# VectorE's order pinned in the attention loops, weight slabs fetched one step ahead, longer spacing in the finish of a group

## The chip, the cores and the metric

The program runs on one core of a Trainium2 chip. Its time is the device time of one execution in microseconds (us). The engines of the core run side by side and wait for each other through semaphores: TensorE (PE) does matmuls and transposes through PSUM, VectorE (DVE) and ScalarE (ACT) do elementwise work, GpSimd (POOL) does a little, and SyncE (SP) issues nearly all DMAs.

## The reference

Four layers run one after the other on x of 2048 tokens by 576 features, in f32: A, B, A, B, each with a residual and a layer norm before it. The two A layers share weights, and so do the two B layers.

```python
def A(x):                                   # attention, one K and one V head for 32 query heads of 18
    q = (x @ wq) per head; k = x @ wk; v = x @ wv
    p = softmax(q k^T * 18**-0.5)           # 32 heads x 2048 x 2048
    return (p v, heads joined) @ wo
def B(x):                                   # linear attention with a learned feature map
    q, k, v = x @ wqkv, 32 heads of 18
    phi(y) = [softmax(y w_phi), softmax(-y w_phi)]          # 36 features
    kv = phi(k)^T v;  z = sum of phi(k)
    return (phi(q) kv / (phi(q) z + 1e-6)) @ wo
x = x + A(norm(x)); x = x + B(norm(x)); x = x + A(norm(x)); x = x + B(norm(x))
```

## The kernel before

**Two attention loops with other work mixed in.** The kernel calls an A layer with the B layer behind it a "layer", so there are two. `attend` holds the loop of one layer. Tokens are cut into 4 chunks of 512 queries, heads into 8 groups of 4. A pair (chunk, group) is one *group* of the loop; the first of 32 is done before the loop, 31 in it. For each group and each of 16 key tiles the loop makes two units: scores of two heads (L451, tile `sc`), their exponential on ScalarE (L963, tile `pt`), and then the product with V, four matmuls (L741). So a group has 32 units, the loop 992.

**The step.** While there is other work ("bulk"), one pass of the loop, here called a step, takes 6 units: `scores(3)`, the sums that are ready, two calls of `tick()`, `scores(3)`, one call of `fill()`, the sums that are ready unless the fill was heavy, and a third `tick()`. `fill()` runs the bulk generator up to the end of one projection (14 matmuls, L205) or up to a `yield STAGE`, which gives the turn back. A step without bulk also takes 6 units and three ticks. 165 steps and a third make the loop.

**The bulk.** For each finished chunk `chunk_work` does 8 projections with `wo` (`output`, residual added by VectorE at L262, `flip_tokens` on VectorE), then `mix` over 4 token tiles: keys b0, b1, values b0, b1, queries b0, b1 (six projections) and `update_state`, 32 small matmuls (L526; the profile counts an f32 matmul twice, so 64 there) whose result VectorE adds to `kv` (L532). After a projection of keys or queries VectorE runs five instructions (`feature_start`, L482 to L487) and ScalarE one exponential (L489); `feature_end` (L494 to L496) normalizes, and the features are block-transposed (L576) and spilled. So a chunk is 36 fills, and 3 of the 4 chunks are done inside the loop; the last follows behind it. In layer 0 the loop's first bulk is `fold_phi`.

**One spare bank.** The loop has two PSUM banks beside those for scores, tags `acc` and `ps`. One collects the group's sum; the other, `Spare`, takes every projection and the state update. When a group ends, the two change places (`homes.reverse()`). So a projection can begin only when VectorE has read the one before it out of the spare bank, and a new group's first sum needs that bank empty too.

**What a tick does.** A tick advances three generators by one `yield`: `urgent` (the finish of a group), `loads` (weight slabs) and `slow` (spills). The finish of a group (`finish_group`): VectorE copies the sums to `osb` (L873); a DMA brings the softmax denominators into `rd`; VectorE takes reciprocals (L881); a DMA writes them to DRAM (`den_rows`), another reads them back spread over the heads (`parts`); VectorE multiplies (L891) and splits the result into a high and a low part; `pack` (L822) moves them into `on` by DMA. `load_weight` brings five slabs of 128 rows through two buffers (`wstage`) and VectorE splits each (L139, L140).

**Who sets the order.** The program is written out by these generators, and a scheduler then orders each engine's instructions by their written place and by its own estimate of the times. In the loops TensorE's order is pinned to the written one: `in_order` chains every PE instruction to the one before. The other engines are ordered by the scheduler. Each engine works strictly in its order; SP too, so a DMA that waits for a semaphore holds every DMA behind it.

**Between the loops.** `last_group` finishes the last group of the loop with transposes instead of DMAs; then come the last chunk's projections, `last_mix`, and the next layer's queries.

Of the kernel before, what the change touches and what calls it, by code (L numbers as in the profile page):

```python
# [60 lines left out]
def kernel(ctx, tc, x_in, wq, wk, wv, wo, wqkv, w_phi, wob, out):  # L61
# [98 lines left out]
    def load_weight(w, src, cols, padded=False, engines=None):  # L160
        hi_engine, lo_engine = engines or (V, V)
        n = cols.stop - cols.start
        hi, lo = w
        for k in range(KT):
            st = stage.tile([P, D], F32, name="wstage")
            if padded:
                nc.sync.dma_start(st[:, :n], src[k * P : (k + 1) * P, cols])
            else:
                for rows, part in row_slot(src, k, cols):
                    nc.sync.dma_start(st[rows, :n], part)  # L170
            split(hi[:, k, :n], lo[:, k, :n], st[:, :n], hi_engine, lo_engine)
            yield STAGE

    w4 = [None, None]
# [673 lines left out]
    def attend(layer, st, a1o, extra, after_chunk, chunks):  # L848
        ctx1 = ExitStack()
        a1 = ctx1.enter_context(tc.tile_pool(name="a1", bufs=2))  # L850
        groups = [(c, g) for c in chunks for g in (*range(NG - 2), NG - 1, NG - 2)]
        qst = {groups[1]: st["q1"]}

        def fetch(n):
            c, g = groups[n]
            qst[c, g] = a1.tile([P, 2, CW], F32R, name="qst")
            load_queries(qst[c, g], layer, c * NG + g)
            load_shifts(qst[c, g], layer, c * NG + g)

        with ctx1:  # L860
            pss = ctx1.enter_context(tc.tile_pool(name="a1s", bufs=3, space=PSUM))
            psm = ctx1.enter_context(tc.tile_pool(name="a1m", bufs=1, space=PSUM))
            homes = [(psa, "acc"), (psm, "ps")]

            class Spare:
                def tile(self, shape, dtype, name):
                    return bank(*homes[1], shape)
            acc, on = {groups[0]: st["acc0"]}, {}
            urgent, bulk, loads, slow = deque(), deque(), deque(), deque()

            def finish_group(c, g):
                osb = a1.tile([P, CW], F32, name="osb", bufs=1)
                V.tensor_copy(osb, acc[c, g])  # L873
                rd = small.tile([P, GH * CW // P], F32, name="rd")
                nc.sync.dma_start(rd, osb[DH::32, :])
                if g == 0:
                    on[c] = a1o.tile([P, 9, CW], F32R, name="on", bufs=1)
                yield STAGE
                yield STAGE
                yield STAGE  # L880
                V.reciprocal(rd, rd)  # L881
                rows = dram.tile([GH, CW], F32, name="den_rows", bufs=2)
                nc.sync.dma_start(rows.rearrange("h (a b) -> (h a) b", b=GH * CW // P), rd)
                yield STAGE
                yield STAGE
                parts = a1.tile([P, 2, CW], F32R, name="parts", bufs=1)
                den = parts[:, 1, :].bitcast(F32)
                nc.sync.dma_start(den, rows[:, None, :].to_broadcast([GH, 32, CW]))
                yield STAGE
                yield STAGE  # L890
                V.tensor_mul(osb, osb, den)  # L891
                split(parts[:, 0, :], parts[:, 1, :], osb, V, V)
                yield STAGE
                yield STAGE
                pack(on[c].bitcast(F32), parts.bitcast(F32), g)
                if g == NG - 2:
                    for _ in range(6):
                        yield STAGE
                    bulk.append(after_chunk(c, on[c], Spare(), loads, slow))
                yield STAGE  # L900

            def values(c, g, t, pt):
                if t == 0:
                    if (c, g) != groups[1]:
                        homes.reverse()
                    acc[c, g] = bank(*homes[0], [P, CW])
                add_values(acc[c, g], t, [pt[j // 2][:, j % 2, :] for j in range(GH)], t == 0, t == NT - 1)
                if t == NT - 1 and (c, g) == groups[-1]:
                    st["last"] = acc[c, g], on[c]
                elif t == NT - 1:  # L910
                    finish(c, g)

            def finish(c, g):
                f = finish_group(c, g)
                next(f)
                urgent.append(f)

            def tick():
                for queue in (urgent, loads, slow):
                    if queue and next(queue[0], DONE) is DONE:  # L920
                        queue.popleft()

            def fill():
                spent = 0
                while bulk:
                    try:
                        v = next(bulk[0])
                    except StopIteration:
                        bulk.popleft()
                        continue  # L930
                    if v is STAGE:
                        break
                    spent += abs(v)
                    if v < 0:
                        break
                return spent

            finish(*groups[0])
            last = [None]

            def in_order():
                for i in traced(nc)[mark[0] :]:
                    if i.engine == mybir.EngineType.PE:
                        if last[0] is not None:
                            tc.add_manual_dep(i, last[0], NOSYNC, reason="order")
                        last[0] = i.name
                mark[0] = len(traced(nc))

            mark = [len(traced(nc))]
            bulk.append(extra(a1, Spare(), loads))  # L950
            units = [(n, t, hh) for n in range(1, len(groups)) for t in range(NT) for hh in range(2)]
            pts, at, done = {}, [0], [0]

            def scores(count):
                ready = at[0] // 2
                for n, t, hh in units[at[0] : at[0] + count]:
                    if t == 0 and hh == 0 and n < len(groups) - 1:
                        fetch(n + 1)
                    sc = pss.tile([P, 2, 512], F32, name="sc")
                    for j in range(2):  # L960
                        score(sc[:, j, :], qst[groups[n]], 2 * hh + j, t)
                    pt = a1.tile([P, 2, 512], F32, name="pt", bufs=3 * BURST)
                    A.activation(pt, sc, AF.Exp, scale=SCALE)  # L963
                    pts[n, t, hh] = pt
                    at[0] += 1
                in_order()
                return ready

            def sums(until):
                while done[0] < until:  # L970
                    n, t, _ = units[2 * done[0]]
                    values(*groups[n], t, [pts.pop((n, t, hh)) for hh in range(2)])
                    done[0] += 1
                    in_order()

            while at[0] < len(units):
                if bulk:
                    sums(scores(BURST))
                    tick()
                    tick()  # L980
                    ready = scores(BURST)
                    spent = fill()
                    in_order()
                    if spent < HEAVY:
                        sums(ready)
                    tick()
                else:
                    for n in range(3):
                        ready = scores(2)
                        sums(min(ready - 1, done[0] + 2))  # L990
                        tick()
            while done[0] < len(units) // 2:
                sums(done[0] + 1)
                tick()
            while urgent:
                tick()
            for queue in (bulk, loads, slow):
                for gen in queue:
                    run(gen)

    BURST = 3
    HEAVY = 1500
    DONE = object()

    def output(c, tt, on, wpo, a1o, ps, copies):
# [5 lines left out]
    def drain(queue):  # L1011
        while queue:
            run(queue.popleft())
# [54 lines left out]
    def chunk_tiles(c):  # L1068
        return range(c * TPC, (c + 1) * TPC)

    chunks = list(range(NC))
    for layer in range(LAYERS):
# [3 lines left out]
        with tc.tile_pool(name="a1o", bufs=2) as a1o:  # L1076
# [29 lines left out]

            def chunk_work(c, on, ps, loads, slow, layer):
                drain(loads)
                tiles = chunk_tiles(c)
                for tt, i in enumerate(tiles):  # L1110
                    yield from output(c, tt, on, st["wo"], a1o, ps, V)
# [122 lines left out]
```

## Time and profile before

| what | us |
|---|---|
| median of 3 runs (lowest, highest) | 2780.73 (2776.71, 2783.16) |
| the profiled execution's own time | 2777.95 |
| its span, first to last instruction | 2776.2 |
| TensorE matmuls busy | 2679.4 (97%) |
| ScalarE busy | 2181.8 (79%) |
| VectorE busy | 1241.8 (45%) |
| mean granted TensorE clock | 0.986 |
| loop of layer 0, layer 1 | 1062.8, 1048.0 |

TensorE is "busy" while a matmul is under way, also while it is held up, so 97% does not say that it works at full speed. The ends of a loop are read from the first and last exponential of L963. The granted clock is 1.00 for most of the loops and falls to half for a few microseconds at a time; a window's column PEclk is the mean over that window.

### The profile page before, as it was taken

What the parts mean: (1) busy time and instruction counts of PE and PEld (TensorE: products, weight loads), DVE (VectorE), ACT (ScalarE), POOL (GpSimd) and SP (SyncE); (2) the same over time, 40 slices, a digit from 0 to 9 for tenths busy, and PEclk for the clock granted to TensorE, in tenths of its full rate; (3) what the DMA queues carried; (4) which work ended last, traced back from release to release, by engine and by line L of the source; (5) the groups of instructions that cost most, each with busy time, mean ns of one, the idle gap of its engine ahead of it and who ended that gap; (6) DMA issues with size and microseconds to landing.
All of it is one profiled execution on the core that took longest, in us unless ns stands there. A gap on an engine that the chain in (4) does not pass through costs nothing. (4 is left out here: it accounts for less than half of the span.)

```text
span 2776.2 us, 55537 instructions
## 1 busy us (share of the span) xinstructions
PE 2679.4 (97%) x22094; PEld 1460.2 (53%) x22094; DVE 1241.8 (45%) x2899; ACT 2181.8 (79%) x2644; POOL 85.9 (3%) x123
## 2 busy tenths in 40 slices
PE   6989999999999999999999999999999999999989
PEld 5733335443454445558987222354535553545788
DVE  7421224444255435558764301144434543454675
ACT  4579998888989989964345899988998998899521
POOL 1000000000000000004000000000000000000110
PEclk9999999999999999999999999999999999999999
DMA  5322232312231223223633311132123212321344
GB/s 186 106 64 65 69 97 59 96 44 61 61 97 48 61 68 98 52 75 117 190 121 99 95 37 35 44 99 58 36 61 103 66 40 66 99 60 43 107 121 139
DMA packets 355814, 224.97 MB, mean 81 GB/s; under 512 B 206874, under 2 KB 288986, under 8 KB 355546
## 3 DMA queue, kind: packets, MB, share of 16 engines
q1 hardware_dynamic: 355546, 221.31, 28.7%
q8 instruction: 178, 2.92, 0.4%
q14 instruction: 90, 0.74, 0.1%
HBM read 132.88 MB, written 67.03 MB: 72 GB/s over the span
## 5 line engine op out<-in xcount | busy, mean ns | idle before, releaser
L963 ACT ACTIVATE pt<-sc 128x1024 f32<-128x1024 f32 x1984 | 1867.9, 1115 | 171.6 <-PE sc L451 152.4
L451 PE MATMUL sc<-qst,kst 56*128 56x512 f32 x3840 | 716.6, 457 | 25.3 <-ACT pt L963 24.2
L451 PEld LDWEIGHTS sc<-qst,kst 56*128 56x128 f32 x3840 | 326.1, 185 | 634.4 <-ACT pt L963 580.7
L741 PE MATMUL acc<-pt,vst 128*32 128x512 f32 x4096 | 510.2, 612 | 6.2 <-DVE kv L532 5.8
L741 PE MATMUL ps<-pt,vst 128*32 128x512 f32 x3840 | 471.8, 599 | 0.8 <-DVE featk L314 0.8
L741 PEld LDWEIGHTS acc<-pt,vst 128*32 128x32 f32 x4096 | 108.9, 111 | 225.0 <-issue 213.0
L741 PEld LDWEIGHTS ps<-pt,vst 128*32 128x32 f32 x3840 | 97.0, 109 | 186.3 <-issue 180.6
L205 PE MATMUL ps<-wahi,xs 128*128 128x288 f32 x783 | 169.9, 303 | 1.0 <-ACT xs L137 0.9
L205 PEld LDWEIGHTS ps<-wahi,xs 128*128 128x128 f32 x783 | 128.1, 188 | 9.4 <-issue 6.5
L205 PE MATMUL ps<-walo,xs 128*128 128x288 f32 x435 | 127.8, 296 | 0.0
L229 POOL TENSOR_TENSOR rstd<-var,neghalf 128x1 f32<-128x1 f32 (+1 forms) x56 | 32.4, 579 | 2490.0 <-DVE var L227 1710.9
L891 DVE TENSOR_TENSOR osb<-osb,parts 128x512 f32<-128x512 f32 x62 | 42.8, 690 | 136.6 <-DMA parts<-den_rows 136.6
L355 PE MATMUL ps<-xsc,wbhi 128*128 128x256 f32 x513 | 97.1, 285 | 5.1 <-DVE xsc L140 2.3
L873 DVE COPY osb<-ps 128x512 f32<-128x512 f32 x30 | 20.7, 689 | 176.6 <-PE ps L741 176.6
L137 ACT ACTIVATE xs<-ps 128x512 fp32r<-128x512 f32 x34 | 20.3, 596 | 92.6 <-PE ps L248 92.4
L205 PE MATMUL ps<-wchi,on 128*128 128x288 f32 x405 | 89.3, 304 | 0.0
L357 ACT ACTIVATE pcs<-ps 128x256 fp32r<-128x256 f32 x71 | 26.6, 384 | 77.0 <-PE ps L355 69.4
L355 PEld LDWEIGHTS ps<-xsc,wbhi 128*128 128x128 f32 x513 | 82.1, 192 | 6.8 <-DVE xsc L140 2.6
L873 DVE COPY osb<-acc 128x512 f32<-128x512 f32 x32 | 22.0, 687 | 142.0 <-PE acc L741 112.5
L205 PE MATMUL ps<-wchi,xs 128*128 128x288 f32 x378 | 83.6, 306 | 0.8 <-DVE wchi L139 0.4
L205 PEld LDWEIGHTS ps<-walo,xs 128*128 128x128 f32 x435 | 81.9, 188 | 0.0
L262 DVE TENSOR_TENSOR xc<-xc,ps 128x288 f32<-128x288 f32 x61 | 27.2, 447 | 118.3 <-PE ps L205 118.3
(320 smaller groups left out, 3549.6 us busy)
## 6 DMA issues: line engine op xcount, KB each, us to landing
qst<-qd SPq DMA_DIRECT2D x360, 72.0 KB
pht<-phi SPq DMA_DIRECT2D x32, 540.0 KB
qd<-pcs SPq DMA_DIRECT2D x64, 256.0 KB
parts<-den_rows SPq DMA_DIRECT2D x62, 256.0 KB
wstage<-folded SPq DMA_DIRECT2D x50, 288.0 KB
on<-parts SPq DMA_DIRECT2D x192, 72.0 KB
phi<-pht SPq DMA_DIRECT2D x96, 144.0 KB
wstage<-in_A_wo_dram SPq DMA_DIRECT2D x32, 288.0 KB
```

The costliest lines, as they stand in the source:

```text
L137: A.activation(dst_hi, src, AF.Copy)
L205: T.matmul(dst, xs[:, slot, :], w[half][:, k, c0 : c0 + HALF], start=(n == 0), stop=(n == last))
L229: G.tensor_tensor(rstd, var, neghalf[:, :n], op=ALU.pow)
L262: V.tensor_add(xr, xr, po)
L355: T.matmul(po, lhs, xsc[:, slot, :], start=(n == 0), stop=(n == LASTP))
L357: A.activation(pc[:, 0, :], po, AF.Copy)
L451: T.matmul(sc, kst[head_rows(h), t * P : (t + 1) * P], q[head_rows(h), h // 2, :], start=True, stop=True)
L741: T.matmul(acc[32 * j : 32 * j + 32, :], vst[:, t, :], pts[j], start=first, stop=last)
L873: V.tensor_copy(osb, acc[c, g])
L891: V.tensor_mul(osb, osb, den)
L963: A.activation(pt, sc, AF.Exp, scale=SCALE)
```

## The change

The set of pinned engines now holds VectorE beside TensorE. `load_weight` issues the fetch of a slab one `yield` before the split that needs it (one more `yield` in all: 6 for 5 slabs). In `finish_group` the spacing between the DMAs grows: 4, 3, 4, 1 ticks (before 3, 2, 2, 2), and the 6 ticks ahead of the next chunk's bulk are replaced by two `yield STAGE` at the start of `chunk_work`, each of which costs that bulk one fill.

```diff
@@ load_weight
-        for k in range(KT):
+        def fetch(k):
             st = stage.tile([P, D], F32, name="wstage")
             if padded:
                 nc.sync.dma_start(st[:, :n], src[k * P : (k + 1) * P, cols])
             else:
                 for rows, part in row_slot(src, k, cols):
                     nc.sync.dma_start(st[rows, :n], part)
+            return st
+
+        st = fetch(0)
+        yield STAGE
+        for k in range(KT):
+            following = fetch(k + 1) if k + 1 < KT else None
             split(hi[:, k, :n], lo[:, k, :n], st[:, :n], hi_engine, lo_engine)
+            st = following
             yield STAGE
@@ finish_group
-                yield STAGE
-                yield STAGE
-                yield STAGE
+                for _ in range(4):
+                    yield STAGE
                 V.reciprocal(rd, rd)
                 rows = dram.tile([GH, CW], F32, name="den_rows", bufs=2)
                 nc.sync.dma_start(rows.rearrange("h (a b) -> (h a) b", b=GH * CW // P), rd)
-                yield STAGE
-                yield STAGE
+                for _ in range(3):
+                    yield STAGE
                 parts = a1.tile([P, 2, CW], F32R, name="parts", bufs=1)
                 den = parts[:, 1, :].bitcast(F32)
                 nc.sync.dma_start(den, rows[:, None, :].to_broadcast([GH, 32, CW]))
-                yield STAGE
-                yield STAGE
+                for _ in range(4):
+                    yield STAGE
                 V.tensor_mul(osb, osb, den)
                 split(parts[:, 0, :], parts[:, 1, :], osb, V, V)
                 yield STAGE
-                yield STAGE
                 pack(on[c].bitcast(F32), parts.bitcast(F32), g)
                 if g == NG - 2:
-                    for _ in range(6):
-                        yield STAGE
                     bulk.append(after_chunk(c, on[c], Spare(), loads, slow))
                 yield STAGE
@@ in_order
-            last = [None]
+            last = {}
             def in_order():
                 for i in traced(nc)[mark[0] :]:
-                    if i.engine == mybir.EngineType.PE:
-                        if last[0] is not None:
-                            tc.add_manual_dep(i, last[0], NOSYNC, reason="order")
-                        last[0] = i.name
+                    if i.engine in PINNED:
+                        if i.engine in last:
+                            tc.add_manual_dep(i, last[i.engine], NOSYNC, reason="order")
+                        last[i.engine] = i.name
+    PINNED = (mybir.EngineType.PE, mybir.EngineType.DVE)
@@ chunk_work
                 drain(loads)
+                yield STAGE
+                yield STAGE
                 tiles = chunk_tiles(c)
```

The changed program has the same instructions on every engine, but for which bank or buffer some of them name; their order differs. Line numbers behind the changed places are some 8 higher in it (L532 becomes L540, L873 L881, L891 L898). TensorE's order outside the loops' bulk is nearly the same. Inside, the bulk of the first and the third chunk stands one step later, that of the second where it stood, and the last state update comes in the last step of the loop instead of the one before it.

VectorE before, layer 0, first chunk, at the second state update (`xs` is the next tile's input, `fz`, `featq` the normalizing of the query features, `osb` the finish of a group, `kv` the state):

```order
L601 CAST xs_6353<-xn_5833 128x128
L487 TENSOR_TENSOR featq_5934<-featq_5934,fmax_6290 128x16x18
L602 TENSOR_TENSOR xs_6353<-xn_5833,xs_6353 64x128
L494 TENSOR_REDUCE fz_6448<-featq_5934 128x32
L873 COPY osb_6334<-ps_5986 128x512
L495 RECIPROCAL fz_6448<-fz_6448 128x32
L496 TENSOR_TENSOR featq_5934<-featq_5934,fz_6448 128x576
L576 STREAM_TRANSPOSE pht_6452<-featq_5934 128x1152
L532 TENSOR_TENSOR kv_2417<-kv_2417,acc_6362 128x288
```

VectorE now, at the same place:

```order
L139 CAST xs_6399<-xn_5884 128x512
L140 TENSOR_TENSOR xs_6399<-xn_5884,xs_6399 128x512
L609 CAST xs_6399<-xn_5884 128x128
L610 TENSOR_TENSOR xs_6399<-xn_5884,xs_6399 64x128
L540 TENSOR_TENSOR kv_2417<-kv_2417,ps_6408 128x288
L502 TENSOR_REDUCE fz_6486<-featq_5981 128x32
L503 RECIPROCAL fz_6486<-fz_6486 128x32
L504 TENSOR_TENSOR featq_5981<-featq_5981,fz_6486 128x576
L502 TENSOR_REDUCE fz_6490<-featq_5981 128x32
L503 RECIPROCAL fz_6490<-fz_6490 128x32
L504 TENSOR_TENSOR featq_5981<-featq_5981,fz_6490 128x576
L584 STREAM_TRANSPOSE pht_6494<-featq_5981 128x1152
```

The addition to `kv` stood behind the normalizing and the transpose, and the copy for a finish stood ahead of it; now it follows the split of the next tile's input, and both halves of the normalizing and the transpose come behind it.

VectorE before, layer 0, second chunk, first tile of `mix` (`wchi`, `wclo` are the slabs of the query weights, `vb` the values b0 and b1 read out of the spare bank):

```order
L139 CAST wchi_8437<-wstage_8542 128x576
L140 TENSOR_TENSOR wclo1_8439<-wstage_8542,wchi_8437 128x576
L873 COPY osb_8582<-ps_8177 128x512
L494 TENSOR_REDUCE fz_8689<-featk_8440 128x32
L495 RECIPROCAL fz_8689<-fz_8689 128x32
L496 TENSOR_TENSOR featk_8440<-featk_8440,fz_8689 128x576
L513 COPY vb0_2419<-acc_8605 128x16x18
L513 COPY vb0_2419<-ps_8673 128x16x18
L881 RECIPROCAL rd_8584<-rd_8584 128x16
L139 CAST wchi_8437<-wstage_8586 128x576
```

VectorE now, at the same place:

```order
L139 CAST wchi_8432<-wstage_8498 128x576
L140 TENSOR_TENSOR wclo0_8433<-wstage_8498,wchi_8432 128x576
L881 COPY osb_8580<-ps_8177 128x512
L139 CAST wchi_8432<-wstage_8540 128x576
L140 TENSOR_TENSOR wclo1_8434<-wstage_8540,wchi_8432 128x576
L139 CAST wchi_8432<-wstage_8584 128x576
L140 TENSOR_TENSOR wclo1_8434<-wstage_8584,wchi_8432 128x576
L521 COPY vb0_2419<-acc_8605 128x16x18
L502 TENSOR_REDUCE fz_8621<-featk_8435 128x32
```

Before, the fifth slab stood behind both copies of the values; now slabs three, four and five all stand ahead of the first of them.

SP before, layer 0, first chunk, around the fetch of the next chunk's residual (`xc`, 1152 KB); `qst` are the next group's queries, `wstage<-folded` the slabs of the query weights:

```order
L94 DMA xd<-xc 128x576 x2
L167 DMA wstage<-folded 128x576 x2
L89 DMA xc<-in_A_x_dram 128x4x576
L440 DMA qst<-qd_104 18x2x512 x6
L445 DMA qst<-mxd_106 2x2x512 x2
L167 DMA wstage<-folded 128x576
L875 DMA rd<-osb 128x1x16
```

SP now, at the same place:

```order
L94 DMA xd<-xc 128x576
L448 DMA qst<-qd_104 18x2x512 x2
L89 DMA xc<-in_A_x_dram 128x4x576
L448 DMA qst<-qd_104 18x2x512 x4
L453 DMA qst<-mxd_106 2x2x512 x2
L168 DMA wstage<-folded 128x576 x3
L883 DMA rd<-osb 128x1x16
```

The fetches of slabs three and four stood ahead of the long transfer; now all of slabs three to five stand behind it and behind the queries.

## The prediction, on record before the changed kernel ran

> **What bounds the kernel now.** I read the page first (busy times), then windows of equal work inside the two loops, then the timeline of the windows that are too long, then the waits.
>
> ```profile
> PE 2679.4 (97%) x22094; PEld 1460.2 (53%) x22094; DVE 1241.8 (45%) x2899; ACT 2181.8 (79%) x2644; POOL 85.9 (3%) x123
> 1702.72:1735.72 33.00, 33.00 (x38) 1.00 0.12 34
> 424.39:464.33 39.94, 34.28 (x36) 1.00 0.24 61
> ...
> sum 2110.80, ACT 1867.87; mean ACT 933.94
> ```
>
> The last row sums two windows, the two loops from the first to the last exponential. The two above it are windows of 36 exponentials of L963, six steps each (the count may take in a neighbour). Without bulk a step takes 33.00/6 = 5.50 us and ScalarE is busy throughout: the exponentials bound it. With a projection in every step it takes 39.94/6 = 6.66 us and ScalarE idles 14%: TensorE bounds it. VectorE, at 45%, bounds neither and matters only where somebody waits for it. Each chunk's bulk is 36 fills, of which four are state updates. So the next windows all hold the same work: a state update's step and the one behind it, twelve exponentials. The first list holds the five such pairs of each layer that are long, the second six of each layer that are not.
>
> ```profile
> 511.07:527.12 16.05, 11.29 (x12) 0.89 0.33 81
> 560.41:578.26 17.85, 11.43 (x13) 0.81 0.37 81
> 657.40:675.17 17.77, 11.16 (x12) 0.81 0.27 60
> ...
> 1922.21:1940.12 17.91, 11.43 (x13) 0.81 0.36 79
> ...
> 2162.01:2175.11 13.10, 11.29 (x12) 1.00 0.41 104
> ...
> sum 158.17, ACT 112.66; mean ACT 11.27
> ```
>
> ```profile
> 611.68:624.15 12.47, 11.32 (x12) 1.00 0.18 45
> ...
> 2528.70:2541.18 12.48, 11.32 (x13) 1.00 0.29 54
> sum 150.01, ACT 135.82; mean ACT 11.32
> ```
>
> A clean pair takes 150.01/12 = 12.50 us, ten long ones 158.17: the excess is 158.17 - 125.0 = 33.2 us. The fourth column is the granted clock: 1.00 in the clean pairs, down to 0.81 in the long ones. One more long step is in layer 1:
>
> ```profile
> 1859.68:1867.71 8.03, 5.71 (x7) 1.00 0.40 118
> 1853.03:1859.68 6.65, 5.72 (x7) 1.00 0.89 294
> ```
>
> It loses 8.03 - 6.65 = 1.4 us. So about 34.6 us of the loops' 2110.8 are stalls, and the rest I take as running at the two paces above. Why the long pairs are long, TensorE first, VectorE behind it (second update, layer 0):
>
> ```profile
> 564.38 0.77 PE L526 MATMUL acc<-featk,vb 128*32 128x36 f32 x64
> 568.07 1.94 PE L741 MATMUL acc<-pt,vst 128*32 128x512 f32 x8 [2.92 <-DVE kv L532]
> 563.87 0.75 DVE L494 TENSOR_REDUCE fz<-featq 128x32 f32<-128x576 f32 x1 [0.67 <-ACT featq L489]
> 564.53 0.68 DVE L873 COPY osb<-ps 128x512 f32<-128x512 f32 x1
> 565.13 0.34 DVE L495 RECIPROCAL fz<-fz 128x32 f32<-128x32 f32 x1
> 565.51 0.76 DVE L496 TENSOR_TENSOR featq<-featq,fz 128x576 f32<-128x576 f32 x1
> 566.30 1.38 DVE L576 STREAM_TRANSPOSE pht<-featq 128x1152 f32<-128x1152 f32 x1
> 567.61 0.42 DVE L532 TENSOR_TENSOR kv<-kv,acc 128x288 f32<-128x288 f32 x1
> ```
>
> The update's matmuls end at 565.15. A new group's sums need the bank that holds them, and the addition that empties it stands behind 2.5 us of normalizing and transposing on VectorE. I call this type a: 560.41 and 1922.21. Type b, first update:
>
> ```profile
> 511.44 0.69 DVE L891 TENSOR_TENSOR osb<-osb,parts 128x512 f32<-128x512 f32 x1 [2.55 <-DMA parts<-den_rows]
> 516.25 0.68 ACT L489 ACTIVATE featq<-featq 128x576 f32<-128x576 f32 x1 [2.31 <-DVE featq L487]
> 517.89 0.50 PE L451 MATMUL sc<-qst,kst 56*128 56x512 f32 x2 [1.19 <-ACT pt L963]
> DVE osb L891 <- DMA parts<-den_rows: 136.6, 50, 6.7
> ```
>
> VectorE stands 2.55 us for a DMA, the query features behind it come late, ScalarE waits for them with all its exponentials queued behind, and TensorE waits for ScalarE. The last row is from the list of waits: VectorE waits so 50 times, 136.6 us in all, and only where an update comes next does it reach TensorE. Six pairs over 14 us remain, this one among them, and I count them all as type b; 801.33 and 2162.01 lose 0.4 and 0.6 us, which I leave as they are.
>
> **What the change does to these, term by term.** Excess by type: a 17.85 + 17.91 - 25.0 = 10.8; small ones 1.0; b the rest, 33.2 - 10.8 - 1.0 = 21.4 us.
>
> *Type a.* With the pin, the addition to `kv` follows the split of the next input, and the copies, normalizing and transpose come behind it (second order in the change). It can start when the matmuls end, and the bulk's shift by a step also moves this update away from the group's start. I take 9.8 of 10.8; bounds 5 (if only the 2.92 of each gap goes) and 10.8.
>
> *Type b.* How much spacing the finish needs:
>
> ```profile
> 503.75 0.38 SPq L883 DMA_DIRECT2D den_rows<-rd  x1
> 788.90 0.48 SPq L167 DMA_DIRECT2D wstage<-folded  x1
> 791.85 0.46 DVE L139 CAST wchi<-wstage 128x576 fp32r<-128x576 f32 x1 [1.44 <-DMA wstage<-folded]
> 783.91 4.24 SPq L445 DMA_DIRECT2D qst<-mxd  x2
> ```
>
> From the issue of `den_rows` (503.75) to the multiply (511.44) 7.7 us pass. Now VectorE's order puts 3 + 4 = 7 ticks there, 7 x 6.66/3 = 15.5 us, twice that; before, the scheduler was free to put the multiply as early as it guessed. SP held up by 4.24 us, as in the last row, still fits. So the waits behind type b go. The same DMAs are issued, and 12 ticks of finish fit into the 16 of a group. I take 18 of 21.4, since the scheduler still places ScalarE's exponentials and some may stand early; bounds 10 and 21.4.
>
> *The long step in layer 1* waits for the fifth slab of query weights; with the pin that slab stands ahead of the values' copies, some steps earlier: 1.4 us, bounds 0 and 1.4.
>
> *Cost 1, slabs inside the bulk.* Three slabs now stand between the keys and the first copy of the values. Cover, from an undisturbed step:
>
> ```profile
> 1810.26 0.40 PE L205 MATMUL ps<-wchi,on 128*128 128x288 f32 x1
> 1812.43 0.45 DVE L262 TENSOR_TENSOR xc<-xc,ps 128x288 f32<-128x288 f32 x1 [2.18 <-PE ps L205]
> 1816.92 0.40 PE L205 MATMUL ps<-wchi,on 128*128 128x288 f32 x1
> 794.17 0.46 DVE L482 COPY featq<-ps 128x288 f32<-128x288 f32 x1 [1.07 <-PE ps L205]
> 796.00 0.46 DVE L487 TENSOR_TENSOR featq<-featq,fmax 128x288 f32<-128x288 f32 x1
> 792.34 0.76 DVE L140 TENSOR_TENSOR wclo<-wstage,wchi 128x576 fp32r<-128x576 f32 x1
> ```
>
> The spare bank is read from 1812.43 on and needed at 1816.92: the read may be 4.5 us late. After the copy of keys b1 at t, VectorE does the feature start (794.17 to 796.46, 2.3 us), slab three (0.46 + 0.76 = 1.2), the finish's copy (0.7), slabs four and five (2.4): done at t + 6.6, when the next projection ends, t + 6.66. The fifth slab's fetch can start when slab three has left its buffer (t + 3.5) and takes 791.85 - 788.90 = 2.95 us, so it lands at t + 6.5, one microsecond after VectorE asks for it: covered by the 4.5. If SP is also held 4.24 us, it lands at t + 10.7 and the read comes 0.9 us too late. Six such places; bounds 0 and 0.9 each; 0.4 each: 2.4 us.
>
> *Cost 2, the loop's end.* The last update comes a step later, so 2 x (0.75 + 0.34 + 0.76) + 1.38 = 5.1 us of VectorE work meet the finish of the last group:
>
> ```profile
> 1226.46 0.69 DVE L832 COPY xn<-acc 128x512 f32<-128x512 f32 x1 [5.03 <-PE acc L741]
> 1231.34 3.36 SPq L822 DMA_DIRECT2D on<-xs  x4
> 1238.58 0.29 PE L205 MATMUL ps<-wchi,on 128*128 128x288 f32 x1
> ```
>
> VectorE idled 5.03 us ahead of this chain. The chain's DMAs are issued by 1234.7 and TensorE needs them at 1238.58, having projected other rows meanwhile: 3.9 us less a landing. Of 5.1 us perhaps 1.5 show at each loop's end: 3 us, bounds 0 and 10.
>
> *No cost:* the 5.1 us behind each update stand ahead of the next projection's copy, which comes a light step (12.50 - 6.66 = 5.8 us) later and may be another 4.5 late; without that cover it would be 12 updates a layer by up to 5 us. The bulk keeps its 108 fills per layer inside 165 steps, so a step's delay exchanges a 5.50 step for a 6.66 one elsewhere. Slab fetches before and between the loops go through the same two buffers in the same order: nothing, bounds -1.4 and 1.4. GpSimd's part is untouched.
>
> Sum: 9.8 + 18 + 1.4 - 2.4 - 3 = 23.8 us. Against the profiled execution's own 2777.95 (2.8 under the median of the three runs, 2780.73): 2754.
>
> **The clock, weighed.** The long pairs lose more than their gaps: 560.41's excess is 5.35 us, TensorE's gap 2.92; the rest goes with PEclk 0.81, about twice the gap. The Trainium skill ("TensorE: Matmul & The Clock Gate", section "Part 1: The HAM clock gate") has the clock fall after at least one idle window of about 3.4 us. Here it fell with a gap of 2.92 us and, in 511.07, with one of 1.19 and shorter ones, so the measurement decides: I count the whole excess.
>
> **The rivals.**
>
> *The clock falls for a reason of its own.* Then only the gaps return, 2.92/5.35 = 55% of the loss: 0.55 x 34.6 = 19 less 5.4 of costs gives 2764. For it: the gaps are short. Against: 1.00 in all twelve clean pairs. 0.06. This is what the 3.4 us of the Trainium skill's page on the clock gate, read strictly, would make of it.
>
> *Half returns.* ScalarE's order is not pinned; an exponential of features that the scheduler puts too early holds the queue as at 516.25. Half of b stays, 9 us: 2754 + 9 + some more cost = 2767. Against: feature instructions now run unmixed, so features come sooner. 0.12.
>
> *No change.* TensorE's order hides VectorE's waits: true for 50 waits of which some six mattered. If as many new ones reach TensorE as go, 2778. 0.09.
>
> *Slower, by the slabs.* VectorE can no longer step around a slab that has not landed: everything behind it, the copy of the values first, waits. For it: all of slabs three to five are now fetched behind the 1152 KB of `xc` (third order), and SP was held there 4.24 us. A late microsecond costs about 1.8 with the clock. To lose the 29.2 us gained and 5.6 more, six places must lose 5.8 each, a gap of 3.2 us: the fifth slab landing 3.2 + 4.5 = 7.7 us after VectorE asks, where I have 1. With SP held twice it would. 2786 and up, 2795 as its middle. 0.11.
>
> **How the numbers follow.** The likeliest case, most stalls gone, has 0.62 and its own range 2741 (all 34.6 and a little more, no cost) to 2764. With the clock and the half case that makes faster 0.80; same (within 0.2%, 5.6 us, about what a measurement of this kernel can tell) 0.09; slower 0.11. Eight in ten reach from 2740 into the top of the half case, 2775.
>
> **What would show it.** Right: the pairs at the updates fall to 12.4 to 13 us with PEclk 1.00; VectorE's wait for `parts` falls from 136.6 us to a few; the `kv` addition starts within 0.5 us of its matmuls; loops some 13 and 16 us shorter. Wrong: VectorE waits of over 4 us for `wstage` ahead of `vb`, TensorE gaps before the values' second projection, or a last group's chain (1226.46 to 1238.58 here) longer than its 12.1 us by more than 3.

## The result, and the profile after

The changed kernel takes 2855.9 us (median of 6 runs, 2849.34 to 2857.5), the kernel before 2781.94 in the same rounds: ratio 1.0263, 95% interval 1.0248 to 1.0279. It is 2.6% slower where 2754 us, 1% faster, was forecast. The profiled execution spans 2855.6 us, the one before 2776.2.

The first row is the line of busy times of the changed kernel, as the prediction's first row is that of the kernel before. The second sums the two loops of the changed kernel, from the first to the last exponential of each; the third does the same for the kernel before (the prediction's 2110.80 was cut 5.8 us wider):

```profile
PE 2692.7 (94%) x22094; PEld 1478.6 (52%) x22094; DVE 1249.9 (44%) x2899; ACT 2182.9 (76%) x2644; POOL 85.2 (3%) x123
...
sum 2172.92, ACT 1869.67; mean ACT 934.84
```

```profile
sum 2104.99, ACT 1867.86; mean ACT 933.93
```

Every engine does the same work; TensorE's share falls because the span grew. Of the 79.4 us between the two spans, 2172.92 - 2104.99 = 67.9 lie in the two loops.

The pairs of steps at the updates, which were the whole gain of the prediction, behave as forecast. These windows of the changed kernel are the ten pairs that took 158.17 us before, the last and their sum:

```profile
...
2363.55:2375.42 11.87, 11.36 (x12) 1.00 0.18 42
sum 123.15, ACT 113.04; mean ACT 11.30
```

The granted clock is 1.00 in all ten: 35.0 us came back. That is 1.8 more than the 33.2 counted as excess, since some of the pairs, like the one shown, are now shorter than the clean 12.50. The loss sits in twelve other steps, two at the start of each mix, which were about 6.66 us long before. First the six just behind the last output projection of a chunk, where TensorE comes to the keys, then the six a step or two later, at the values:

```profile
480.62:497.31 16.69, 5.71 (x7) 0.70 0.26 70
...
2468.34:2482.68 14.34, 5.71 (x7) 0.81 0.50 147
sum 92.67, ACT 34.27; mean ACT 5.71
```

```profile
504.12:516.98 12.86, 5.71 (x6) 0.78 0.59 178
...
2482.68:2493.97 11.29, 5.71 (x6) 0.80 0.59 144
sum 75.43, ACT 34.25; mean ACT 5.71
```

At 6.66 us each, the first six lose 92.67 - 40.0 = 52.7 us, the second 75.43 - 40.0 = 35.5: 88.2 together.

**The first hold.** The timeline of the first such step, SyncE, then VectorE, then TensorE (line numbers are those of the changed kernel: L830 the pack, L895 the fetch of `parts`, L898 the multiply, L213 a projection):

```profile
470.70 2.00 SPq L587 DMA_DIRECT2D flipped<-pht  x4
480.11 3.40 SPq L830 DMA_DIRECT2D on<-parts  x4
...
485.40 0.58 SPq L895 DMA_DIRECT2D parts<-den_rows  x1
...
490.46 0.69 DVE L898 TENSOR_TENSOR osb<-osb,parts 128x512 f32<-128x512 f32 x1 [16.53 <-DMA parts<-den_rows]
```

```profile
479.79 0.29 PE L213 MATMUL acc<-wclo,on 128*128 128x288 f32 x1
...
492.75 0.61 PE L213 MATMUL acc<-wahi,xs 128*128 128x288 f32 x1 [8.07 <-DVE xc L270]
```

Read from the first row: SyncE issues nothing from 472.70 to 480.11. What it then issues is the pack of the *next* chunk's first group into `on`, and the last matmul that reads the old `on` ended at 480.08. `on` has one buffer. Behind the pack stands the second group's fetch of `parts`, due since its 7 ticks were up, issued at 485.40 and landed 5 us later. VectorE, in its fixed order, stands 16.53 us at the multiply; the addition to `xc` that empties the spare bank comes behind it; TensorE stops for 8.07 us.

The other five places go the same way: SyncE stands 7.3 to 7.8 us, the pack is issued within 0.04 us of the end of the last read of `on`, and VectorE waits 10.7 to 16.7 us at the multiply. In four of the six TensorE then waits for the copy of the keys, which also stands behind the multiply, and not for `xc`. One thing stays open: `parts` has a single buffer too, and the pack reads it, so the fetch would have to wait for the pack even if SyncE were free. No run separates the queue from the buffer.

**The second hold.** Then SyncE has a backlog, and VectorE meets the third slab:

```profile
496.39 2.22 SPq L587 DMA_DIRECT2D flipped<-pht  x4
...
501.07 0.40 SPq L89 DMA_DIRECT2D xc<-in_A_x_dram  x1
501.51 1.61 SPq L448 DMA_DIRECT2D qst<-qd  x4
...
503.85 8.26 SPq L168 DMA_DIRECT2D wstage<-folded  x3
```

```profile
510.51 0.46 DVE L139 CAST wchi<-wstage 128x576 fp32r<-128x576 f32 x1 [4.61 <-DMA wstage<-folded]
...
511.69 0.68 DVE L881 COPY osb<-ps 128x512 f32<-128x512 f32 x1
...
514.56 0.46 DVE L139 CAST wchi<-wstage 128x576 fp32r<-128x576 f32 x1 [1.03 <-DMA wstage<-folded]
...
512.42 0.61 PE L213 MATMUL ps<-wbhi,xs 128*128 128x288 f32 x1 [4.24 <-DVE osb L881]
```

The buffer of the third slab was free at 499.97, when the first had been split. Its fetch is issued 3.9 us later, behind this row of transfers, and lands at 510.5, 6.7 us after its issue, beside the 1152 KB of `xc`. So late a landing is found in the first chunk of each layer alone, where the fetch is issued 2.8 us behind `xc` (6.7 and 5.7 us to land); in the other four places it is issued 8.0 us behind `xc` and lands after 3.0 to 3.4 us, and what is left is the late issue. VectorE waits for it with the copy to `osb` behind it: a group ends here, the two banks change places, and TensorE can project the second half of the values only into the bank that this copy empties. A group's end falls into all six of these steps. In four TensorE waits for the copy to `osb`; in the two at 97 steps into a loop the new group's sums need the bank that still holds the values:

```profile
803.47 5.13 PE L749 MATMUL acc<-pt,vst 128*32 128x512 f32 x24 [5.22 <-DVE vb L521]
```

### The profile page after: what moved, and what is told of

Same layout as the page of the kernel before. It is cut to its first block, busy times and chain, and to the rows that moved or that the text cites. A ratio compares the mean times of both kernels' runs of the same rounds, so it can differ in the third digit from the quotient of the medians.

```text
span 2855.6 us, 55566 instructions
## 1 busy us (share of the span) xinstructions
PE 2692.7 (94%) x22094; PEld 1478.6 (52%) x22094; DVE 1249.9 (44%) x2899; ACT 2182.9 (76%) x2644; POOL 85.2 (3%) x123
## 5 line engine op out<-in xcount | busy, mean ns | idle before, releaser
L213 PE MATMUL ps<-wahi,xs 128*128 128x288 f32 x747 | 162.8, 304 | 1.1 <-ACT xs L137 0.9
L213 PEld LDWEIGHTS ps<-wahi,xs 128*128 128x128 f32 x747 | 122.7, 189 | 8.0 <-issue 3.8
L213 PE MATMUL ps<-walo,xs 128*128 128x288 f32 x415 | 122.4, 297 | 0.0
L213 PE MATMUL acc<-wahi,xs 128*128 128x288 f32 x288 | 71.9, 336 | 41.0 <-DVE featk L490 24.7
L213 PE MATMUL ps<-wbhi,xs 128*128 128x288 f32 x378 | 86.6, 315 | 12.8 <-DVE osb L881 12.8
L898 DVE TENSOR_TENSOR osb<-osb,parts 128x512 f32<-128x512 f32 x62 | 42.5, 685 | 122.9 <-DMA parts<-den_rows 122.9
L881 DVE COPY osb<-acc 128x512 f32<-128x512 f32 x32 | 22.1, 690 | 163.2 <-PE acc L749 131.8
L213 PE MATMUL ps<-wchi,on 128*128 128x288 f32 x387 | 86.5, 308 | 0.0
L213 PEld LDWEIGHTS acc<-wahi,xs 128*128 128x128 f32 x288 | 53.6, 214 | 52.2 <-DVE featk L490 26.4
```

What stands on the lines that cost most here:

```text
L213: T.matmul(dst, xs[:, slot, :], w[half][:, k, c0 : c0 + HALF], start=(n == 0), stop=(n == last))
```

## The experiments

Two theories. **P, the pack**: SyncE's wait for `on` reaches VectorE through the fetch of `parts`. **S, the slabs**, the prediction's own rival: VectorE can't step around a slab that has not landed.

**One step sooner.** One of the two `yield STAGE` at the head of `chunk_work` is taken out.

> The changed kernel with one of the two steps taken out that the change put ahead of a chunk's bulk, so that the output projections start and end one step (6.65 us) earlier. Theory P, the pack: the first group's pack into `on` waits on SyncE until the old chunk's last output projection has read `on`; the second group's fetch of `parts` stands behind it on SyncE, and VectorE, in its fixed order, stands at the multiply that needs it. The six long steps that start so lose 92.7 - 6 x 6.65 = 52.8 us; a step earlier, the fetch lands before the multiply, and most of it goes: 2803 if the slab steps stay as long as they are (35.6 us over), 2765 to 2775 if they were long only because SyncE worked off what had piled up. Theory S, the slabs: VectorE stands for the third to fifth slab, which are fetched behind `xc` whatever the step: 2840 to 2856.

Measured 2847.19 us, 1.0234 (1.0217 to 1.0251): a miss for P, and inside the range given for S. The profile shows the pack released at 471.8 instead of 480.1, as P has it, but VectorE still waits:

```profile
477.63 0.58 SPq L895 DMA_DIRECT2D parts<-den_rows  x1
...
483.12 0.69 DVE L898 TENSOR_TENSOR osb<-osb,parts 128x512 f32<-128x512 f32 x1 [10.86 <-DMA parts<-den_rows]
```

I had moved the release by a step and forgotten what follows it on SyncE: pack, `flipped`, `xn`, then the fetch, then its landing, 11.3 us in all. The wait fell from 16.53 to 10.86, still far over what TensorE has cover for, and the bulk, now sooner, met its own `on` before it had landed (TensorE waited 2.91 us for that transfer at 718.25). So P's wait had not been taken away, and the time decides nothing between P and S; the next two runs do.

**Slabs free; multiply free; both.** Instructions named in `free` are left out of VectorE's chain:

```diff
+            start = len(traced(nc))
             split(hi[:, k, :n], lo[:, k, :n], st[:, :n], hi_engine, lo_engine)   # slabs
+            free.update(i.name for i in traced(nc)[start:])
...
+                start = len(traced(nc))
                 V.tensor_mul(osb, osb, den)                                       # multiply
                 split(parts[:, 0, :], parts[:, 1, :], osb, V, V)
+                free.update(i.name for i in traced(nc)[start:])
...
-                    if i.engine in PINNED:
+                    if i.engine in PINNED and i.name not in free:
```

> The changed kernel with the slabs' splits left out of the fixed order, so that VectorE may step around a slab that has not landed; everything else on VectorE stays pinned. Theory P: the wait at the multiply stays, only part of the 35.6 us of the slab steps goes: 2820 to 2850. Theory S: nearly all that was lost comes back: 2760 to 2790.

> The changed kernel with three instructions of a group's finish left out of VectorE's fixed order (the multiply of `osb` by `parts` and the split behind it); the slabs' splits stay pinned. Theory P+S, two separate holds: the steps that start at the multiply go (52.8 us in the changed kernel, 61 with the slabs free), those at the slabs stay (35.6): 2795 to 2806. Theory P alone, where slabs are late only because SyncE works off what the pack held up: 2765 to 2780. Theory S alone: 2845 and up.

> The changed kernel with both left out of the fixed order, the slabs' splits and the finish's multiply with its split; all else on VectorE stays pinned. P+S: 88 to 95 us come back and the gains at the updates stay: 2760 to 2772, under the 2774.5 of the kernel with nothing pinned on VectorE, since the additions to `kv` stay early. If the scheduler places the freed multiply in front of the features again, half of those gains go: 2772 to 2782. If a third hold takes the place of the two: above 2800.

Measured: slabs free 2830.32 (1.0184, 1.0167 to 1.0201), multiply free 2838.49 (1.0206, 1.019 to 1.0222), both 2794.15 (1.0044, 1.003 to 1.0057). The sums of the same two lists of six steps, slabs free and then multiply free:

```profile
sum 101.14, ACT 34.27; mean ACT 5.71
...
sum 39.82, ACT 34.27; mean ACT 5.71
```

```profile
sum 41.35, ACT 34.30; mean ACT 5.72
...
sum 110.11, ACT 34.50; mean ACT 5.75
```

Each edit takes away exactly its own six steps (39.8 and 41.4 are clean) and the other six get longer, by 8.5 and by 34.7 us; that is why the multiply free missed its 2795 to 2806. So both holds are real, and one covers the other: with the multiply out of the way VectorE arrives sooner at the slab (at 495.6, not 505.9), whose fetch is still behind SyncE's row of transfers:

```profile
502.69 7.43 SPq L170 DMA_DIRECT2D wstage<-folded  x3
...
508.52 0.46 DVE L139 CAST wchi<-wstage 128x576 fp32r<-128x576 f32 x1 [12.96 <-DMA wstage<-folded]
...
510.43 0.61 PE L215 MATMUL ps<-wbhi,xs 128*128 128x288 f32 x1 [12.60 <-DVE osb L883]
```

Both free took longer than expected (2760 to 2772, or 2772 to 2782 with the multiply in front of the features). The scheduler puts the freed multiply into the middle of the query features, and type b of the prediction is back, as here; how much of the 22 us over 2772 this makes was not counted:

```profile
1072.93 0.69 DVE L903 TENSOR_TENSOR osb<-osb,parts 128x512 f32<-128x512 f32 x1 [3.02 <-DMA parts<-den_rows]
...
1074.03 0.68 ACT L501 ACTIVATE featq<-featq 128x576 f32<-128x576 f32 x1 [3.04 <-DVE featq L499]
```

**The parts of the change by themselves.** Without the pin (`PINNED` holds TensorE alone); before with the pin alone; before with the spacing alone; before with the slabs alone.

> The changed kernel with VectorE's order left to the scheduler again; spacing and slabs a step ahead stay. Both theories: VectorE can step around what has not landed, so the 88 us of long steps go: 2765 to 2790. If it stays above 2830, neither theory holds, since both need the fixed order.

> The kernel before with nothing but VectorE's order pinned; its spacing and its slab loading stay. Theory P: in the kernel before, the pack was issued at 470.5 and `parts` landed by 480.1, with the multiply due 7 ticks (15.5 us) behind the copy at about 457, so VectorE stands some 7.6 us there, 3 more than TensorE has cover for: six places of about 6 us with the clock, against some 10 us of gain at the additions to `kv`: 2790 to 2815. Theory S: each slab's split stands right behind its own fetch, so every load has five waits of about 3 us in VectorE's way, which is worse than with the slabs a step ahead: above 2850.

> The kernel before with nothing but the new spacing (more steps between the transfers of a finish, and the bulk a step later): no pin, slabs as before. The kernel with spacing and slabs a step ahead, without the pin, gained 0.3%. If that is the spacing, 2768 to 2776; if it is the slabs, 2779 to 2785.

> The kernel before with nothing but the slabs fetched a step ahead: no pin, spacing as before. If the slabs make the 0.3%, 2770 to 2777; if the spacing does, 2779 to 2785.

Measured against the kernel before: without the pin 2774.47 (0.997, 0.9953 to 0.9987); pin alone 2874.15 (1.0329, 1.0312 to 1.0346); spacing alone 2770.53 (0.9963, 0.9949 to 0.9976); slabs alone 2786.21 (1.0009, 0.9995 to 1.0022), 1.2 us over the 2785 expected at most. The pin makes the whole loss, about 81 us on top of the other two and 93 by itself; the spacing makes a small gain; the slabs a step ahead make no measurable difference. P was too low on the pin alone (2790 to 2815): it took a wait of 7.6 us at the multiply, the first such wait is 16.46 us, and in all there are 255.7 us in 38 waits, in the row below, against 136.6 in 50 before. The time lies where S had it, above 2850, and VectorE's waits for the slabs of the query weights grew too, from 11.9 us in 6 to 41.5 in 10: both holds are in this kernel.

```profile
DVE osb L891 <- DMA parts<-den_rows: 255.7, 38, 21.4
```

**Taking away what is late, with the order still fixed.** The pack of a chunk's first group is issued with the second group's, with two buffers for `parts`; four slab buffers, with four slabs fetched ahead of the last output projections; both; both, with the fetch of `xc` written behind the mix.

```diff
-                pack(on[c].bitcast(F32), parts.bitcast(F32), g)
+                if g == 0 and c != chunks[0]:
+                    held.append((on[c], parts))
+                else:
+                    while held:
+                        first = held.pop()
+                        pack(first[0].bitcast(F32), first[1].bitcast(F32), 0)
+                    pack(on[c].bitcast(F32), parts.bitcast(F32), g)
...
+                    if tt == 3:
+                        slabs = fetch_slabs(scratch[0])
                     yield from output(c, tt, on, st["wo"], a1o, ps, V)
...
-                loads.append(load_wpq())
+                loads.append(load_wpq(slabs=slabs))
```

> The changed kernel, all pinned as it is, but the pack of a chunk's first group is issued together with the second group's, and `parts` has two buffers: no SyncE instruction that waits for the old chunk's output projections stands ahead of the second group's fetch of `parts`. P+S: the wait at that multiply goes (52.8 us), but nine transfers of about 0.85 us each now stand on SyncE ahead of the third slab, so the slab steps grow as they did with the multiply freed (by 46 us over the changed kernel's): 2835 to 2850. If the pack's wait for `on` was the only reason for late slabs: 2770 to 2805. If the wait at the multiply had another reason: above 2850.

> The changed kernel, all pinned as it is, with four slab buffers; four of the five slabs of query weights are fetched ahead of the last output projections of a chunk, the fifth when the first is split. P+S: the slab steps shrink, the steps at the multiply stay, as with the slabs freed: 2825 to 2840. S alone: 2765 to 2780.

> Both of the last two kernels in one: VectorE's order fully fixed, and neither the pack nor the first four slabs can hold what it waits for. P+S: the 88 us go and the gains at the updates stay, less what the fifth slab (fetched behind `xc` and the queries) still costs: 2758 to 2785. If SyncE's order makes a third hold of the same size: above 2800.

> The kernel of both, with the fetch of `xc` moved behind the mix in the written order, so that the fifth slab isn't issued behind its 1152 KB. If `xc` was what made the fifth slab late, 5 to 20 us less than the kernel of both; if the queries and their shifts on SyncE do, within 5 us of it.

Measured: pack held 2806.26 (1.0085, 1.0067 to 1.0103), slabs ahead 2814.99 (1.0113, 1.0093 to 1.0133), both 2764.4 (0.9939, 0.9924 to 0.9953), both with `xc` later 2763.82 (0.9933, 0.992 to 0.9947). The lists of six steps, in this order: pack held, slabs ahead, both:

```profile
sum 39.95, ACT 34.29; mean ACT 5.71
...
sum 77.85, ACT 34.26; mean ACT 5.71
```

```profile
sum 92.33, ACT 34.27; mean ACT 5.71
...
sum 40.96, ACT 34.28; mean ACT 5.71
```

```profile
sum 39.98, ACT 34.30; mean ACT 5.72
...
sum 39.99, ACT 34.27; mean ACT 5.71
```

With both, all twelve steps are clean though nothing was taken out of VectorE's order, and the wait at the multiply is down to 69.4 us in 15 waits from 122.9 in 15. That is the mechanism, shown from the side of its cause. Two forecasts missed. Slabs ahead is 10 us under its 2825 to 2840, which was not followed up. With the pack held the slab steps grew by 2.4 us only, not 46: SyncE still stands until 480.06 in that kernel, but then the two packs go out one behind the other and are done at 487.42, so the third slab's fetch is issued at 495.01, 8.8 us sooner than in the changed kernel.

In the kernel of both, VectorE still waits for the fifth slab, six times, with no TensorE time lost in the twelve steps; from its list of waits, and the first of them:

```profile
DVE wchi L139 <- DMA wstage<-folded: 8.7, 6, 3.4
...
499.13 0.46 DVE L139 CAST wchi<-wstage 128x576 fp32r<-128x576 f32 x1 [3.38 <-DMA wstage<-folded]
```

That slab was issued at 492.29, 3.0 us behind `xc`, and landed 6.8 us later. With `xc` written behind the mix it is issued at 489.35 and is there when VectorE comes to it at 494.69; none of the six waits is left, and the time is the same. So a slab fetched close behind `xc` does land later, here by 1.5 us at least, and in this kernel that costs nothing.

**Is the pin worth anything there?** The kernel of both, with VectorE left to the scheduler.

> The fastest kernel so far (pack of the first group issued with the second's, four slabs ahead, all of VectorE pinned) with VectorE's order left to the scheduler. If the pin itself gains once nothing late stands in its order, this is slower than 2764.4: 2768 to 2778, with the long pairs of the updates back. If that gain came from the buffers and the spacing alone, the same within 0.2%: 2759 to 2767.

Measured 2765.24 (0.9943, 0.9929 to 0.9958): the same as 2764.4 within 0.2%. The ten update pairs, with the pin and without it:

```profile
sum 123.67, ACT 112.87; mean ACT 11.29
```

```profile
sum 132.98, ACT 112.41; mean ACT 11.24
```

The pin does shorten the pairs, by 9.3 us, and gives it back elsewhere, 6.1 us of it at the step described below under "No cost", which takes 10.40 and 9.03 us in the pinned kernel of both; and of the 34.5 us between the 158.17 of before and 123.67, 25.2 come without it.

## Why the prediction was wrong, point by point

**The step that failed** is type b's sentence on spacing: "SP held up by 4.24 us, as in the last row, still fits. So the waits behind type b go." It took the time from the issue of `den_rows` to the multiply from a place where SyncE was free and added the one hold that the trace of before showed. In that trace the pack is also issued only when the last output projection has read `on`:

```profile
470.14 0.29 PE L205 MATMUL acc<-wclo,on 128*128 128x288 f32 x1
...
470.47 3.36 SPq L822 DMA_DIRECT2D on<-parts  x4
...
475.59 0.57 SPq L888 DMA_DIRECT2D parts<-den_rows  x1
```

and VectorE went on with slabs and key features until 480.80, where the multiply stood. The chain was there to be read; what hid it was the freedom that the change took away. "12 ticks of finish fit into the 16 of a group" counts one group's finish and not its neighbour, whose pack waits for another chunk's reader. Missing cost: 52.7 us. Two of the prediction's own signs of being wrong came true, a wait of 4.61 us for `wstage` ahead of `vb` and a gap of 4.24 us before the values' second projection, and one sign of being right did not: the wait for `parts` is 122.9 us in 15 waits, not a few.

**Cost 1, slabs inside the bulk**, was mis-sized: 2.4 us forecast, 0 to 0.9 for each of six places; measured 35.5, 5.9 each. The hold on SyncE was priced about right (4.24 us taken, 3.9 measured above), but the working lets it fall on the fifth slab and takes the third as landed; VectorE waits 4.61 us for the third and 1.03 for the fifth. What failed above all is the cover, "the read may be 4.5 us late", taken from an undisturbed step (and counted from the start of a read of 0.45 us, so that 4.0 are left). A group ends in each of the six places, and there the bank that is read late is wanted at once. The working even counts "the finish's copy (0.7)", and not what waits for it. The Trainium skill ("Perfetto Trace Analysis", section "What 'DMA-bound' means") lists the issuing engine's sequencer, solid with DMA slices, as a limit of its own; the trace comes near that in SyncE's stretch from 496.39 to 503.75, in which it is busy for 6.0 of 7.4 us.

**The rival "Slower, by the slabs"** had the right sign, with a chance of 0.11. Its 5.8 us a place was what it needed to come out slower at all, not a forecast, and it expected the fifth slab to be late; that 5.9 were measured beside it is luck. By itself it would have made 2754 + 33 = 2787; the rest is the pack, which no rival had. Its reason, 1152 KB of `xc` in front, holds in part in two of the six places, where the third slab took 6.7 and 5.7 us to land.

**Types a and b** were right in their result: 29.2 us forecast of the ten pairs and the long step, 35.0 measured in the pairs alone, clock 1.00. The attribution was half wrong. Spacing and the later bulk bring most of it without the pin: the same ten pairs in the kernel with the spacing alone are 27.7 us shorter than before.

```profile
sum 130.52, ACT 112.44; mean ACT 11.24
```

The update that met a group's start (560.41 before) leaves it by the shift of a step. The prediction named that shift in half a sentence and gave the gain to the pin.

**No cost** missed one place. Behind an update that falls at a group's end, the 5.1 us of normalizing and transposing stand between the copy to `osb` and the next keys' copy:

```profile
1123.66 0.69 DVE L881 COPY osb<-acc 128x512 f32<-128x512 f32 x1 [3.77 <-PE acc L749]
...
1128.07 1.38 DVE L584 STREAM_TRANSPOSE pht<-featq 128x1152 f32<-128x1152 f32 x1
1129.37 0.42 DVE L490 COPY featk<-ps 128x288 f32<-128x288 f32 x1
...
1129.84 4.08 PE L749 MATMUL ps<-pt,vst 128*32 128x512 f32 x24 [2.32 <-DVE featk L490]
```

Once a layer: 10.34 and 9.03 us instead of 6.66, 6.1 together. The named cover was the light step; the group's end took it.

**Cost 2, the loop's end**: 3 us forecast, bounds 0 and 10. The stretch between the loops grew by 4.0 us and the tail by 5.5, 9.5 in all. The transpose of the last features does stand inside the last group's chain, at 1269.02, and that chain's pack is issued 6.3 us after the copy (4.9 before). But from the end of a loop to the first addition to `xc` the stretches grew by no more than 0.9 and 3.0 us, and in the kernel with the spacing alone, where the pack follows the copy by 4.9 and 5.3 us, they grew by 0.7 and 2.1. That kernel has 1.7 of the 4.0 between the loops and 5.0 of the tail's 5.5, so most of the 9.5 is not the pin; its cause stays open.

The sum as it came out: 35.0 us came back; lost were 52.7, 35.5, 6.1 and 9.5, another 2.0 ahead of the first loop and 8.6 in steps of 7.0 to 7.4 us and others that I did not follow. That is 79.4 us slower.

## What to carry to other kernels

Pinning an engine's order hands it every wait of the queues that feed it: before doing so, follow each transfer that a pinned instruction needs back along the issuing queue, past whatever stands in front of it there, to the reader that frees its destination. A wait that costs nothing under a free order is no evidence that it costs nothing under a fixed one. Remove the late thing (buffers, an earlier fetch, a later pack) rather than the order; once that was done here, the pin was worth nothing measurable, and 0.6% came from the buffers, the order of transfers and the spacing.

## What the hardware showed that I had not expected

The prediction priced a late microsecond at 1.8 with the clock. Here it is not a factor. The gaps of 4.24, 8.07 and 12.60 us shown above stand in steps of 12.86, 16.69 and 21.22 us (the last in the row below, of the kernel with the multiply free), which is 6.2, 10.0 and 14.6 over 6.66: the gap and 2.0 us each time.

```profile
493.76:514.98 21.22, 5.71 (x6) 0.68 0.57 165
```

Over all twelve long steps of the changed kernel, whose gaps are 2.6 to 8.2 us, it is the gap and 1.6 to 2.4 us. At shorter gaps it is not regular: the two steps under "No cost" have a gap of 2.32 us each, and one takes 1.4 us more than its gap, at a clock of 0.83, the other nothing more, at 1.00. The matmuls of the changed kernel show where the 2.0 come from:

```profile
478.33 0.43 PE L213 MATMUL acc<-wchi,on 128*128 128x288 f32 x2
...
493.40 0.69 PE L213 MATMUL acc<-wahi,xs 128*128 128x288 f32 x2
...
497.85 2.78 PE L749 MATMUL ps<-pt,vst 128*32 128x512 f32 x24
```

A pair takes 0.69 us instead of 0.43 from the restart at 492.75 until about 497.85, and then all is as before: in these steps a restart costs the same after 4 us as after 12. The Trainium skill ("TensorE: Matmul & The Clock Gate", section "Part 1: The HAM clock gate") has the clock back after at least one busy window of about 3.4 us; the 5.1 us here are over that, and agree with it.
